# One core: another order of the steps in pooled attention with two gated MLPs

## The chip, the core and the metric

The kernel runs on one core of one Trainium2 chip. The metric is the device time of one execution in microseconds. In the views of the profile PE is TensorE's matrix unit, PEld its weight loads, DVE is VectorE, ACT is ScalarE, POOL is GpSimd and SP is SyncE, which issues the DMAs. A span runs from the first instruction to the last.

## The reference

Three stages follow one another on 8 batches of 576 rows and 512 columns.

```python
# attention, 8 heads of 64: keys and values are means over 8 rows (576 -> 72)
scores = scale * np.matmul(q, k_p.transpose(0, 1, 3, 2))
scores = scores - np.max(scores, axis=-1, keepdims=True)
attn = np.exp(scores)
attn = attn / (np.sum(attn, axis=-1, keepdims=True) + 1e-09)
x = np.matmul(attn, v_p)                  # then heads side by side
# first MLP, 512 -> 1024 -> 512
h = np.maximum(x @ w_in, 0.0)
conv_out = ...                            # 3 taps along the rows, per column
x = h * (1.0 / (1.0 + np.exp(-conv_out))) @ w_out
# second MLP, 512 -> 2 x 512 -> 512
h = gelu_tanh(x @ w_in)
u, v = (h[..., :d_ff // 2], h[..., d_ff // 2:])
v_n = (v - mu) / np.sqrt(var + 1e-06) * g_ln
v_s = np.einsum('ts,bsd->btd', w_sg, v_n) + b_sg[None, :, None]
out = x + (u * v_s) @ w_out
```

## The kernel before

**Precision.** Every large product is made from high and low parts: a tile is cast on ACT to the short form, the rest is subtracted into a second tile (`subtract`, L134, on DVE or POOL), and three matmuls take the place of one (`mm3`, L99 to L101, `mm_sum`, L106, `three` and `passes`, L746). Some weights arrive as 64-bit numbers; `to_f32` makes f32 of them with three DVE instructions on integers (L146, L149, L152).

**Tasks.** The work is cut into tasks, each a generator of steps. A step is named by the letter of its task, an index and a batch, as `u1.4`. For the places below:

- `k`, `K`, `v`, `V`: load and pool keys and values; `p`, `q`: transposes of q (DVE, L403); `s`: scores and softmax (matmuls L418, DVE L431); `e`: transposes of the exponentials and their split (ACT cast L502, L134); `a`: attention output.
- `i`, `t`: loads and conversions of the weights of the first MLP; `I`: its input product (PE L106 into `psi`), relu (ACT L557), taps (ACT L567, DVE L569 and L570), tanh (ACT L572), gate (DVE L576), cast and low part (ACT L579, POOL L134); `O`: its output product (PE L99 to L101 into `pso`, evacuated at L601 and L603 into `ob`, stored to `x2s` in DRAM).
- `y` (`t_x2`): the stored result is loaded as `xb` (SP, L675) and transposed by DVE (L681, two halves). `T` (`t_xc`): for seven products, a POOL subtraction of quarters (L693), an ACT cast (L698) and the low part (L134).
- `n` and `u` (`t_v2`, `t_u`): the second MLP's products for v and u, each with seven products instead of eight (Strassen and Winograd's scheme). `products` sets their steps: matmuls 1, 5, copy, 6, 2, copy, 7, add, copy, 4, add, 3 and the last evacuations. Three ACT copies (L769 for `n`, L813 for `u`, into `tmp`) must be made before the next product is accumulated in the same bank; three DVE adds (L774, L823) and gelus on ACT (L771, L777, L778, L820, L826, L827) close it. For v follow statistics on DVE (L783, L784), the inverse deviation on POOL (L787, L788) and the normalisation on DVE (L791, two of 128x512).
- `g`, `G`, `H`, `l`: the spatial weights and the last ones (conversions by `to_f32`). `S` (`t_sc`): quarters of v for the spatial product (POOL L927, ACT L616, DVE L134). `d` (`t_sp`): the spatial product with the same scheme, its evacuations on DVE (L976) and the multiplication with u on POOL (L980). `o`: the output product and the residual.

**Banks.** PSUM has three banks called `psa`, two `psi` and three `pso`, so a product waits until the bank's earlier user has been evacuated.

**Order.** A string `ORDER` with 3617 keys lists the steps. The function `step` advances the generator of a key by one step and ties each instruction that this issues to the one before on the same engine:

```python
        for n in range(seen[0], len(issued)):
            ins = issued[n]
            if ins.engine in last:
                tc.add_manual_dep(ins, last[ins.engine], pin, reason="order")
            last[ins.engine] = ins.name
```

So the string alone sets the order on every engine's queue, SP's with its DMAs among them. Between engines only data and buffers order the work.

Of the kernel before, what the change touches and what calls it, by code (L numbers as in the profile page):

```python
# [26 lines left out]
def pooled_attention_gated_mlps(  # L27
# [25 lines left out]
    B, H, S, D = q.shape  # L53
# [35 lines left out]
    def a_bank():  # L89
        return psum1.tile([128, 512], F32, tag="a", bufs=3, name="psa")  # L90
# [45 lines left out]
    def to_f32(raw, t, tmp=None):  # L136

        w = raw.rearrange("p (n t) -> p t n", t=2)
        lo, up = w[:, 0, :], w[:, 1, :]
        ti = t.bitcast(U32)
        mi = ti if tmp is None else tmp.bitcast(U32)
        nc.vector.tensor_scalar(out=mi, in0=up, scalar1=3, scalar2=0x3FFFFFF8,  # L146
                                op0=ALU.logical_shift_left, op1=ALU.bitwise_and)
        yield
        nc.vector.scalar_tensor_tensor(out=mi, in0=up, scalar=0xC0000000, in1=mi,  # L149
                                       op0=ALU.bitwise_and, op1=ALU.bitwise_or)  # L150
        yield
        nc.vector.scalar_tensor_tensor(out=ti, in0=lo, scalar=29, in1=mi,  # L152
                                       op0=ALU.logical_shift_right, op1=ALU.bitwise_or)
        yield
# [82 lines left out]
    def staged(name, n, where=None):  # L237

        if where is not None:
            p_, tag, size = where  # L240
            early[name] = [p_.tile([128, size], F32, tag=tag, name=name), 0]
        z, at = early[name]
        early[name][1] += 512 * n
        return z[:, at:at + 512 * n].rearrange("p (a s) -> p a s", a=n)

    def pool_sum(eng, raw, dst, n):
        a = raw[0:n]
        if eng is nc.vector:
            eng.tensor_reduce(out=dst, in_=a.rearrange("p a (r d) -> p a d r", r=POOL), axis=AX.X, op=ALU.add)
            return  # L250
        eng.tensor_tensor(out=a[:, :, 0:256], in0=a[:, :, 0:256], in1=a[:, :, 256:512], op=ALU.add)
        yield
        eng.tensor_tensor(out=a[:, :, 0:128], in0=a[:, :, 0:128], in1=a[:, :, 128:256], op=ALU.add)
        yield
        eng.tensor_tensor(out=dst, in0=a[:, :, 0:64], in1=a[:, :, 64:128], op=ALU.add)

    kv = {}

    def t_k(i, b):

        n = (2, 2, 1)[i]
        P = 128 if i < 2 else 64
        if b > 1:
            raw = att2.tile([128, 2, 512], F32, tag="raw", name="raw")
        else:
            raw = staged(f"st{b}", n, ((in1, "xh", XW * KC), (slot, "hg", 2 * NF * CH))[b] if i == 0 else None)
        rows_ = k[b].rearrange("h (j r) d -> (h j) (r d)", r=POOL)[256 * i:256 * i + P * n]
        nc.sync.dma_start(out=raw[0:P, 0:n], in_=rows_.rearrange("(a p) x -> p a x", p=P))
        yield
        if b == 1:  # L270
            kv["k1", i] = raw
            return
        if ("kp", b) not in kv:
            kv["kp", b] = att1.tile([128, 5, D], F32, tag="kp", name="kp")
        eng = dve if b == 0 and i != 1 else pool
        yield from pool_sum(eng, raw[:, 0:n], kv["kp", b][0:P, 2 * i:2 * i + n, :], P)
# [332 lines left out]
    w2 = {}  # L609
# [15 lines left out]
    wf, wc = {}, {}  # L625

    def t_w2(i, *_):
        kt, e = i % KC, i // KC
        p = w2["p"]
        raw = p.tile([128, 1024], U32, tag=f"c{e}{4 + kt % 3}", name="w2raw")  # L630
        for c in range(4):
            r0 = 128 * c + 32 * kt
            nc.sync.dma_start(out=raw[32 * c:32 * c + 32], in_=w_in2[r0:r0 + 32, 1024 * e:1024 * e + 1024])
        yield
        if kt % 2 == 0:
            wf[e, kt // 2] = p.tile([128, 2, 512], F32, tag=f"c{e}{kt // 2}", name="w2f")
        yield from to_f32(raw, wf[e, kt // 2][:, kt % 2, :], a_bank())
# [301 lines left out]
    g2 = {}  # L939
# [112 lines left out]
    def step(key):  # L1052

        if key not in running:
            i, _, b = key[1:].partition(".")
            running[key] = iter(tasks[key[0]](int(i or 0), int(b or 0)) or ())
        more = next(running[key], 0)
        issued = nc.cur_bb.bb.instructions
# [5 lines that stand above are left out]
        seen[0] = len(issued)  # L1064
        return more is None

    for key in ORDER.split():
        step(key)
# [30 lines left out]
```

## Time and profile before

| What | Value |
|---|---|
| median of 3 runs | 979.6 us |
| lowest, highest | 978.8, 980.35 us |
| profiled execution | 980.6 us |
| its span | 978.8 us |
| its mean granted clock of TensorE | 0.988 |
| PE busy | 925.9 us (95%) |
| DVE busy | 785.7 us (80%) |
| POOL busy | 564.1 us (58%) |
| ACT busy | 530.4 us (54%) |

The span falls into stages: the opening with the first batch's attention and the loads of weights (0 to 57 us), the start of the first MLP (57 to 137), its steady part (137 to 540), the passage to the second MLP (540 to 577), the products for u and v (577 to 760), the start of the spatial gating (760 to 800), its steady part and the end (800 to 979). A share of busy time over the whole span mixes these, so the views below are read by stage. In the view of windows a granted clock of 1.00 is 2.4 GHz and 0.50 is 1.2 GHz.

### The profile page before, as it was taken

How to read it: one execution, taken by the hardware profiler on the slowest of the kernel's cores; microseconds unless marked ns; L12 is line 12 of the kernel's file. 1: busy time of each engine (PE TensorE's matmuls, PEld its weight loads, DVE VectorE, ACT ScalarE, POOL GpSimd, SP SyncE). 2: the span in 40 equal slices, each digit the busy share in tenths (PEclk: the TensorE clock that was granted, in tenths of full speed). 3: DMA queues.
4: the chain of work that ended last, by engine and by line, in shares of the span. 5: the costliest groups of instructions: out<-in, count | busy, mean ns of one | idle time of the engine just before them, and what ended most of it. 6: DMA issues, size and time to landing. Idle time of an engine off the chain costs nothing.

```text
span 978.8 us, 15842 instructions
## 1 busy us (share of the span) xinstructions
PE 925.9 (95%) x5396; PEld 843.8 (86%) x5396; DVE 785.7 (80%) x1399; ACT 530.4 (54%) x1108; POOL 564.1 (58%) x630
## 2 busy tenths in 40 slices
PE   5888899999999999999999899999999899999998
PEld 5677789989898998988899689998899889989996
DVE  5889997879788688787877469898786889797774
ACT  3656677676667576675656356655556333233211
POOL 3777797777968575475253265643653655554430
PEclk9899999999999999999999999999999999999999
DMA  9975183646746255132710685476437565566453
GB/s 236 266 225 98 47 182 105 156 142 155 186 112 164 85 138 137 49 95 68 198 40 1 121 166 131 137 209 149 124 125 231 187 211 180 148 213 185 163 175 129
DMA packets 182701, 143.61 MB, mean 147 GB/s; under 512 B 99776, under 2 KB 136924, under 8 KB 182620
## 3 DMA queue, kind: packets, MB, share of 16 engines
q1 hardware_dynamic: 182620, 142.61, 54.0%
q8 instruction: 42, 0.69, 0.3%
q14 instruction: 39, 0.32, 0.1%
HBM read 94.20 MB, written 48.37 MB: 146 GB/s over the span
## 4 chain that ended last, share of the span: by engine, by line
PE 68%; DVE 14%; DMA 8%; SPq 4%; issue 3%; ACT 2%; POOL 2%; DVEq 0%; ACTq 0%; POOLq 0%
PE psi L106 18%; PE psa L746 9%; PE pso L746 8%; PE pso L99 6%; PE pso L101 6%; PE pso L100 6%; PE psi L100 3%; PE psi L99 3%; PE psi L101 3%; DMA xb<-x2s 3%; PE psa L418 3%; PE psa L106 3%; DMA st<-in_v_dram 1%; DMA qb<-in_q_dram 1%; DVE sc L134 1%
## 5 line engine op out<-in xcount | busy, mean ns | idle before, releaser
L134 POOL TENSOR_TENSOR hg<-g,hg 128x384 fp32r<-128x384 f32 x96 | 100.9, 1057 | 77.9 <-ACT hg L579 77.2
L980 POOL TENSOR_TENSOR u<-u,tmp 128x288 f32<-128x288 f32 x64 | 61.1, 971 | 76.7 <-DVE tmp L976 67.6
L569 DVE SCALAR_TENSOR_TENSOR psi<-h,coef,psi 128x384 f32<-128x384 f32 x96 | 58.9, 614 | 31.3 <-ACT psi L567 30.7
L557 ACT ACTIVATE h<-psi 128x386 f32<-128x386 f32 (+1 forms) x96 | 47.4, 493 | 56.8 <-PE psi L106 56.5
L693 POOL TENSOR_TENSOR xb<-xb 128x768 f32<-128x768 f32 x24 | 45.7, 1905 | 47.5 <-DVE xc L134 21.4
L572 ACT ACTIVATE psi<-psi 128x384 f32<-128x384 f32 x96 | 46.0, 480 | 47.7 <-DVE psi L570 47.2
L134 POOL TENSOR_TENSOR eTl<-xb,eTh 128x512 fp32r<-128x512 f32 (+1 forms) x30 | 46.4, 1545 | 43.9 <-ACT eTh L502 41.4
L616 ACT CAST sc<-vf 128x512 fp32r<-128x512 f32 x48 | 28.9, 619 | 63.3 <-POOL vf L927 29.0
L570 DVE SCALAR_TENSOR_TENSOR psi<-h,coef,psi 128x384 f32<-128x384 f32 x96 | 59.8, 623 | 3.4
L576 DVE SCALAR_TENSOR_TENSOR g<-psi,h 128x384 f32<-128x384 f32 x96 | 52.2, 544 | 11.4 <-ACT psi L572 9.5
L418 PE MATMUL psa<-KBT,qT 128*128 128x144 f32 (+1 forms) x320 | 53.5, 300 | 7.0 <-DVE e L431 2.8
L418 PEld LDWEIGHTS psa<-KBT,qT 128*128 128x128 f32 (+1 forms) x320 | 45.0, 184 | 15.4 <-issue 5.7
L567 ACT ACTIVATE psi<-h,coef 128x384 f32<-128x384 f32 x96 | 56.3, 586 | 3.1
L579 ACT CAST hg<-g 128x384 fp32r<-128x384 f32 x96 | 47.7, 506 | 15.2 <-DVE g L576 13.7
L746 PE MATMUL psa<-xc,wc 128*128 128x384 f32 x252 | 51.5, 350 | 4.5 <-DVE xc L134 2.4
L746 PE MATMUL pso<-wc,xc 128*128 128x256 f32 x378 | 52.0, 285 | 3.8 <-POOL xc L134 2.1
L746 PE MATMUL psa<-wc,xc 128*128 128x256 f32 x378 | 51.7, 284 | 3.7 <-ACT tmp L769 2.3
L746 PEld LDWEIGHTS pso<-wc,xc 128*128 128x128 f32 x378 | 49.0, 190 | 5.2 <-ACT tmp L769 2.5
L746 PEld LDWEIGHTS psa<-wc,xc 128*128 128x128 f32 x378 | 49.1, 189 | 4.8 <-ACT tmp L769 3.1
L746 PE MATMUL pso<-xc,wc 128*128 128x384 f32 x252 | 48.6, 338 | 3.3 <-ACT tmp L813 2.0
L746 PEld LDWEIGHTS psa<-xc,wc 128*128 128x128 f32 x252 | 44.8, 196 | 6.5 <-DVE xc L134 2.7
L995 ACT CAST g<-u 128x256 fp32r<-128x256 f32 x64 | 22.1, 403 | 45.8 <-POOL u L980 35.2
(396 smaller groups left out, 3130.1 us busy)
## 6 DMA issues: line engine op xcount, KB each, us to landing
xb<-eds SPq DMA_DIRECT2D x24, 384.0 KB, 3.1
x2s<-ob SPq DMA_DIRECT2D x36, 256.0 KB, 2.3
xb<-x2s SPq DMA_DIRECT2D x48, 192.0 KB, 5.1
us<-ub SPq DMA_DIRECT2D x24, 384.0 KB, 2.7
vs<-vg SPq DMA_DIRECT2D x18, 512.0 KB, 4.8
u<-us SPq DMA_DIRECT2D x16, 576.0 KB, 5.9
vf<-vs SPq DMA_DIRECT2D x16, 512.0 KB, 4.2
out_dram<-ob SPq DMA_DIRECT2D x32, 256.0 KB, 2.5
```

The costliest lines, as they stand in the source:

```text
L99: nc.tensor.matmul(out=out_, lhsT=ah, rhs=bh, start=first, stop=False)
L100: nc.tensor.matmul(out=out_, lhsT=al, rhs=bh, start=False, stop=False)
L101: nc.tensor.matmul(out=out_, lhsT=ah, rhs=bl, start=False, stop=last)
L106: nc.tensor.matmul(out=out_, lhsT=a, rhs=b_, start=(i == 0), stop=(i == n - 1))
L134: eng.tensor_tensor(out=out, in0=in0, in1=hi.bitcast(F32), op=ALU.subtract)
L418: nc.tensor.matmul(out=ps[0:n, 2 * SP * x:2 * SP * x + 2 * SP], lhsT=qT[:, p, 0:n], rhs=KBT[:, p, :], start=True, stop=True)
L567: nc.scalar.activation(out=y, in_=tap(1), func=AF.Copy, scale=cw(1, f))
L569: nc.vector.scalar_tensor_tensor(out=y, in0=tap(0), scalar=cw(0, f), in1=y, op0=ALU.mult, op1=ALU.add)
L570: nc.vector.scalar_tensor_tensor(out=y, in0=tap(2), scalar=cw(2, f), in1=y, op0=ALU.mult, op1=ALU.add)
L576: nc.vector.scalar_tensor_tensor(out=go, in0=y, scalar=1.0, in1=tap(1), op0=ALU.add, op1=ALU.mult)
L746: nc.tensor.matmul(out=ps, lhsT=a, rhs=b_, start=first and i == 0, stop=last and i == n - 1, skip_group_check=True)
L980: pool.tensor_tensor(out=z, in0=z, in1=o, op=ALU.mult)
```

## The change

The string `ORDER` is replaced by one with the same 3617 steps in another order; the steps of one task keep their own sequence. Every engine runs the same instructions as before (PE 5148, DVE 1399, ACT 1106, POOL 627 and SP 625 in the program). Most steps move by a few places. Two more edits issue no instruction: in `t_k` a tile is noted before the first pause of the step instead of after it, and in `t_w2` a tile is made by whichever of two steps comes first; they let some steps stand in another order. Lines below them have a number higher by one in the changed kernel.

```diff
-ORDER = '''z k0.0 k1.0 k2.0 z z p0.0 c p1.0 p2.0 v0.0 v1.0 p3.0 p4.0 v2.0 i0 i1 z z k0.1 k1.0 p0.1 t3 k0.0 p0.0 k1.0 i2
...
+ORDER = '''z k0.0 k1.0 k2.0 z z p0.0 c p1.0 p2.0 v0.0 v1.0 p3.0 p4.0 v2.0 i0 i1 z z k0.1 p0.0 p0.0 i3 p0.1 k1.0 k1.0 k1.0
...
@@ t_k @@
-        yield
         if b == 1:
             kv["k1", i] = raw
+        yield
+        if b == 1:
             return
...
@@ t_w2 @@
-        if kt % 2 == 0:
+        if (e, kt // 2) not in wf:
```

Three places follow. A row is an instruction with the tiles that it writes and reads; a number behind a name tells tiles of that name apart.

**The transition.** On DVE, where the second MLP's first input `xb` is transposed and split into `xc`, before:

```order
L681 STREAM_TRANSPOSE xb_6118<-xb_6118 128x768 x2
L681 STREAM_TRANSPOSE xb_6126<-xb_6126 128x768
L134 TENSOR_TENSOR xc_6132<-xb_6118,xc_6132 128x768
L681 STREAM_TRANSPOSE xb_6126<-xb_6126 128x768
L134 TENSOR_TENSOR xc_6164<-xb_6118,xc_6164 128x768
L134 TENSOR_TENSOR xc_6198<-xb_6118,xc_6198 128x768
L843 STREAM_TRANSPOSE wsg_6178<-wsg_6178 128x576
```

and now:

```order
L682 STREAM_TRANSPOSE xb_6102<-xb_6102 128x768 x2
L134 TENSOR_TENSOR xc_6135<-xb_6102,xc_6135 128x768
L682 STREAM_TRANSPOSE xb_6110<-xb_6110 128x768 x2
L134 TENSOR_TENSOR xc_6158<-xb_6102,xc_6158 128x768
L134 TENSOR_TENSOR xc_6161<-xb_6102,xc_6161 128x768
L602 TENSOR_SCALAR ob_6206<-pso_6080 128x512
L844 STREAM_TRANSPOSE wsg_6208<-wsg_6208 128x576
```

The low part of the first split stands between the transposes of the two halves of the input instead of behind three of them, and the evacuation of the output product (L602) stands ahead of the weights' transpose.

**The products, at 684 to 690 us of the trace.** On DVE, with the statistics and normalisation of v (`vg`), the adds of u (`ub`) and the input of the next batch (`xb`, `xc`), before:

```order
L784 BN_AGGR mv_7584<-st_7583 128x2
L681 STREAM_TRANSPOSE xb_7461<-xb_7461 128x768
L823 TENSOR_TENSOR ub_7621<-pso_7574,tmp0_7551 128x384
L134 TENSOR_TENSOR xc_7618<-xb_7531,xc_7618 128x768
L791 TENSOR_SCALAR vg_7414<-vg_7414,mv_7584,rstd_7623 128x512 x2
L774 TENSOR_TENSOR vg_7589<-psa_7638,tmp0_7610 128x256
L823 TENSOR_TENSOR ub_7662<-pso_7521,tmp2_7626 128x384
```

and now:

```order
L785 BN_AGGR mv_7596<-st_7595 128x2
L134 TENSOR_TENSOR xc_7611<-xb_7553,xc_7611 128x768
L824 TENSOR_TENSOR ub_7614<-pso_7568,tmp0_7551 128x384
L792 TENSOR_SCALAR vg_7413<-vg_7413,mv_7596,rstd_7601 128x512 x2
L682 STREAM_TRANSPOSE xb_7537<-xb_7537 128x768
L775 TENSOR_TENSOR vg_7579<-psa_7626,tmp0_7616 128x256
L775 TENSOR_TENSOR vg_7579<-psa_7604,tmp2_7649 128x256
```

The last transpose of `xb` has moved from ahead of the normalising pair to behind it, and the statistics that stood between the transposes are further ahead. On ACT at 711 to 717 us, with the copies of u's bank (L813, now L814) and the cast of the next input (L698, now L699), before:

```order
L813 COPY tmp0_7918<-psa_7904 128x384
L698 CAST xc_7927<-xb_7920 128x768
L813 COPY tmp1_7951<-psa_7904 128x384
L771 ACTIVATE vg_7824<-pso_7825 128x256
L777 ACTIVATE vg_7824<-vg_7824 128x256
```

and now:

```order
L814 COPY tmp0_7925<-psa_7906 128x384
L814 COPY tmp1_7940<-psa_7906 128x384
L699 CAST xc_7949<-xb_7895 128x768
L772 ACTIVATE vg_7820<-pso_7821 128x256
L814 COPY tmp2_7962<-psa_7906 128x384
```

The second copy has passed the cast, and the third one the gelu at L778. On PE five of the pairs in which the product 4 stood right behind the product 7 of the same bank have other products between them, and three such pairs are new.

**The start of the spatial gating.** On DVE from 770 to 778 us, with the evacuations L976 (now L977), the low parts of the spatial input (`sc`) and a weight conversion (L146), before:

```order
L976 SCALAR_TENSOR_TENSOR tmp_8638<-pso,coef,bsg 128x288
L976 SCALAR_TENSOR_TENSOR tmp_8638<-pso,coef,tmp_8638 128x288
L976 SCALAR_TENSOR_TENSOR tmp_8581<-pso,coef,bsg 128x288
L134 TENSOR_TENSOR sc<-vf,sc 128x512
L976 SCALAR_TENSOR_TENSOR tmp_8626<-psa,coef,tmp_8626 128x288
L134 TENSOR_TENSOR sc<-vf,sc 128x512
L976 SCALAR_TENSOR_TENSOR tmp_8546<-psa,coef,bsg 128x288
L134 TENSOR_TENSOR sc<-vf,sc 128x512
L976 SCALAR_TENSOR_TENSOR tmp_8611<-pso,coef,tmp_8611 128x288
L146 TENSOR_SCALAR t<-T4raw 128x512
L134 TENSOR_TENSOR sc<-sf,sc 128x512
```

and now:

```order
L977 SCALAR_TENSOR_TENSOR tmp_8638<-pso,coef,bsg 128x288
L977 SCALAR_TENSOR_TENSOR tmp_8638<-pso,coef,tmp_8638 128x288
L134 TENSOR_TENSOR sc<-sf,sc 128x512
L134 TENSOR_TENSOR sc<-vf,sc 128x512
L977 SCALAR_TENSOR_TENSOR tmp_8585<-pso,coef,bsg 128x288
L134 TENSOR_TENSOR sc<-vf,sc 128x512
L977 SCALAR_TENSOR_TENSOR tmp_8632<-psa,coef,tmp_8632 128x288
L134 TENSOR_TENSOR sc<-vf,sc 128x512
L977 SCALAR_TENSOR_TENSOR tmp_8529<-psa,coef,bsg 128x288
L134 TENSOR_TENSOR vr<-vf,vr 64x512
L977 SCALAR_TENSOR_TENSOR tmp_8587<-psa,coef,tmp_8587 128x288
L146 TENSOR_SCALAR t<-T4raw 128x512
```

The low part that is taken from `sf` has moved to the front, behind the second evacuation into `tmp`, and the conversion L146 stands further back. On SP the loads of the next batch's v for the gating now stand ahead of the loads of the residual.

Elsewhere: in the opening one weight load of the first MLP's output side (`t3`) moves back behind others, some (`i3`, `i5`, `i6`) move forward, and two DVE instructions (a coefficient's and a weight's) move back. In the start of the first MLP the scores' product `s0.1` stands before a block of the input product on PE, and the DVE transpose of `p2.2` stands ahead of two attention steps. In the steady part of the first MLP one gate (`I6.9`) moves forward, and one (`I1.7`) now stands behind a subtraction of the exponentials (`e0.6`) on DVE.

## Rows read from the trace of the kernel before

**Rows 1.** Windows: window, length, busy PE, PEld, DVE, ACT, POOL, clock, DMA share

```profile
0.00:30.00 30.00, 18.52 (x121) 15.81 (x122) 19.66 (x40) 12.20 (x30) 12.46 (x32) 0.95 1.07 247
30.00:57.00 27.00, 24.59 (x166) 20.59 (x166) 21.49 (x41) 17.03 (x44) 20.36 (x26) 0.86 1.06 280
57.00:137.00 80.00, 69.79 (x412) 60.73 (x410) 76.31 (x141) 50.67 (x110) 61.42 (x84) 1.00 0.49 109
137.00:540.00 403.00, 400.87 (x2138) 363.23 (x2139) 326.92 (x597) 267.13 (x535) 261.38 (x310) 1.00 0.45 118
540.00:577.00 37.00, 31.02 (x143) 26.59 (x142) 18.62 (x23) 13.97 (x24) 17.45 (x11) 0.91 0.73 134
577.00:760.00 183.00, 172.89 (x1191) 168.46 (x1191) 152.00 (x258) 109.91 (x229) 89.53 (x75) 1.00 0.56 159
760.00:800.00 40.00, 34.77 (x225) 32.27 (x224) 37.12 (x68) 12.40 (x28) 21.39 (x21) 0.96 0.56 173
800.00:979.00 179.00, 173.48 (x1011) 156.16 (x1009) 133.56 (x237) 47.05 (x114) 80.08 (x74) 0.99 0.56 177
```

**Rows 2.** The same windows view around TensorE's half clock

```profile
27.20:34.10 6.90, 6.80 (x38) 5.28 (x38) 5.74 (x12) 5.13 (x15) 5.03 (x9) 0.51 1.11 224
774.80:778.20 3.40, 1.43 (x11) 1.19 (x9) 3.40 (x5) 1.13 (x3) 3.40 (x4) 1.00 0.23 83
778.20:781.60 3.40, 3.02 (x12) 3.02 (x13) 3.37 (x5) 0.62 (x3) 3.40 (x3) 0.50 0.00 0
```

**Rows 3.** Waits of PE in 577 to 760: total us, times, longest

```profile
PE psa L746 <- ACT tmp L769: 2.3, 4, 0.7
PE pso L746 <- ACT tmp L813: 2.0, 3, 1.0
PE psa L746 <- DVE vg L774: 1.5, 1, 1.5
```

**Rows 4.** Timeline: start, length, engine, line, tiles, idle before and releaser; 677 to 691

```profile
677.01 0.99 DVE L791 TENSOR_SCALAR vg<-vg,mv,rstd 128x512 f32<-128x512 f32 x2
...
686.89 2.49 DVE L791 TENSOR_SCALAR vg<-vg,mv,rstd 128x512 f32<-128x512 f32 x2
687.05 4.02 POOL L693 TENSOR_TENSOR xb<-xb 128x768 f32<-128x768 f32 x2 [1.15 <-DVE xc L134]
...
690.23 0.96 PE L746 MATMUL pso<-xc,wc 128*128 128x384 f32 x4 [1.32 <-DVE ub L823]
```

**Rows 5.** Timeline, ACT and PE, 714 to 717

```profile
714.75 0.83 ACT L698 CAST xc<-xb 128x768 fp32r<-128x768 f32 x1 [3.21 <-DVE xb L681]
...
716.02 1.15 PE L746 MATMUL psa<-xc,wc 128*128 128x384 f32 x5 [1.21 <-ACT tmp L813]
```

**Rows 6.** Timeline, DVE and PE, 772 to 779

```profile
772.22 0.52 DVE L976 SCALAR_TENSOR_TENSOR tmp<-pso,coef,bsg 128x288 f32<-128x288 f32 x1 [1.50 <-POOL u L980]
...
777.24 1.28 DVE L134 TENSOR_TENSOR sc<-sf,sc 128x512 fp32r<-128x512 f32 x1
...
778.58 1.57 PE L746 MATMUL psa<-sgc,sc 128*128 128x288 f32 x5 [2.35 <-DVE sc L134]
```

**Rows 7.** Timeline of the transition: DVE, POOL and PE

```profile
554.68 0.98 DVE L681 STREAM_TRANSPOSE xb<-xb 128x768 f32<-128x768 f32 x1 [1.99 <-DMA xb<-x2s]
...
557.66 2.40 POOL L693 TENSOR_TENSOR xb<-xb 128x768 f32<-128x768 f32 x1 [1.83 <-DMA wsg<-in_moe_w_sg_dram]
...
568.43 0.86 PE L746 MATMUL pso<-wc,xc 128*128 128x256 f32 x5 [2.13 <-POOL xc L134]
```

**Rows 8.** Waits of PE in 57 to 137

```profile
PE psa L418 <- DVE e L431: 2.8, 2, 2.3
PE psa L418 <- DVE qT L403: 2.2, 1, 2.2
```

**Rows 9.** Timeline, DVE, 57 to 60

```profile
57.43 2.48 DVE L146 TENSOR_SCALAR t<-w0raw 128x512 uint32<-128x512 uint32 x1 [1.73 <-POOL wi6hl L134]
```

**Rows 10.** Timeline, DVE, 366 to 371

```profile
366.89 3.51 DVE L134 TENSOR_TENSOR eTh<-xb,eTh 32x256 fp32r<-32x256 f32 x1
```

More of the change, by code (lines that the diff above doesn't have):

```diff
@@ L268, in t_k @@
         nc.sync.dma_start(out=raw[0:P, 0:n], in_=rows_.rearrange("(a p) x -> p a x", p=P))
+        if b == 1:
+            kv["k1", i] = raw
         yield
         if b == 1:
-            kv["k1", i] = raw
             return
```

2 lines of the change are left out of this document (1 added, 1 removed).

## The prediction

> **What bounds the kernel now.** I read the profile in this order: busy time of each engine by stage, the granted clock of TensorE around its pauses, what PE waits for in each stage, and then the timeline at the longest of those waits.
>
> The stages [rows 1] show PE as the bound nearly everywhere: it is busy for 400.87 of 403 us in the steady part of the first MLP, 172.89 of 183 in the products of the second, and 173.48 of 179 in the spatial gating. The change adds and removes no instruction, so PE's busy time at full clock stays, and there are only two things to win: time in which PE stands still, and time in which it runs at half clock. Length less busy time gives PE's idle time by stage: 11.5 us in 0–30, 2.4 in 30–57, 10.2 in 57–137, 2.1 in 137–540, 6.0 in 540–577, 10.1 in 577–760, 5.2 in 760–800 and 5.5 after, 53 us in all. Two stages have another bound beside PE: in 57–137 the DVE is busy for 76.31 of 80 us, and in 760–800 for 37.12 of 40. There PE waits because DVE is full, so a swap helps only if it makes DVE's work shorter or brings forward the one result that PE lacks.
>
> The clock adds to it. After PE was busy for 1.43 of 3.40 us, the next 3.40 us ran at a granted 0.50, that is 1.2 GHz instead of 2.4 [rows 2]; 6.90 us of the opening ran at 0.51. Half of a 3.4 us stretch in which PE works all the time is 1.7 us lost, on top of the wait before it. PE was at work for 3.02 us of that gated stretch, so it cost some 1.5.
>
> **The change part by part.** Every engine runs its instructions in the order of the steps, so a step that moves takes all that it issues with it. The sum is made against the profiled execution (980.6 us, span 978.8), which lies 1.0 above the median of 979.6.
>
> *The products, 577–760.* PE's waits there [rows 3] are mostly for evacuations, the copies of ACT and the adds of DVE that free a PSUM bank. Three of them stand behind something that had no need to go first.
> First [rows 4]: PE starts at 690.23 after 1.32 us of waiting for DVE's add L823, which stood behind the normalising pair L791. That pair takes 0.99 us where POOL is quiet (677.01) and took 2.49 at 686.89, with POOL's subtractions L693 starting at 687.05: 1.50 us more. POOL could begin because DVE had done the last transpose for them just before. In the new order that transpose comes behind the pair, so POOL cannot have begun when the pair runs. The add then ends some 1.5 us sooner and the 1.32 goes.
> Second [rows 5]: ACT's copy that PE awaits at 716.02 (1.21 us) stood behind the cast at 714.75, which had itself waited 3.21 us for DVE's transposes. The new order has the copy in front of the cast: 1.21 goes. Third, PE's longest wait for a copy of L813 into the other bank, 1.0 [rows 3]: this copy now precedes two gelus on ACT, and 1.0 goes. Together 3.5 us.
> Smaller ones: four waits for the copies of L769 make 2.3 us [rows 3]; PE waits about half a microsecond wherever a product that needs the copy of a bank stands directly behind the product before it in that bank. Five such pairs get other products between them (−2.5 at 0.5 each) and three new ones arise (+1.5): −1.0. The remaining moves of this stage bring waits and take them, at about this size; I put them at zero. Term −4.5; from −8, if the 1.5 us wait on L774 [rows 3] and 2 us of the small ones go too, to 0, if each wait is replaced.
>
> That a DVE instruction with two SBUF inputs and a POOL instruction delay one another is shown by [rows 4]. The Trainium skill, "SBUF — State Buffer", section "Who interferes with whom", gives the reason as a port pair that one instruction holds to its end, and adds that whichever issues first holds it: the order of issue decides who is blocked. The 2.49 against 0.99 agrees with that. This rule also speaks against the change: the order is fixed within each engine only, and which of two engines comes first is decided on the chip. By it the 1.32 could come back at the next pair, and the term would be −3.2 instead of −4.5.
>
> *Spatial gating begins, 760–800.* PE waits 2.35 us at 778.58 for the low part of a split that DVE makes at 777.24, and then runs 3.4 us at half clock [rows 2, 6]. DVE had been idle for 1.50 us before 772.22, and the inputs of that low part were there. In the new order it stands ahead, in this idle time, and the weight conversion L146 comes later. The wait and its half-clock stretch are worth 2.35 + 1.5 = 3.9 us. But DVE has only 2.9 us of idle time in this stage [rows 1]; 1.50 of it is now filled by work that left a full stretch, so DVE gets 1.5 us ahead, and what is next late is a later L976. I take half of the 3.9: −2. Bounds: −4.5 (the wait, the stretch and a little more) and +1 (POOL is at work in just that idle time, and a meeting costs 1.50 as in [rows 4]).
> On SP's queue the next batch's loads go ahead of the residual loads here; those are needed 30 us later and their transfer costs nothing.
>
> *The transition, 540–577.* DVE waited 1.99 us for a load at 554.68 [rows 7]; the low part of the first split now fills this, and the second transposes come about 1 us sooner, with them POOL's subtraction at 557.66 (from there 10.8 us of POOL, ACT and DVE work in series lead to PE's product at 568.43, which waited 2.13). On PE two blocks of the output projection now stand before the first product instead of behind: that moves the waits and takes none away. Term −1, the 1 us on the serial chain; −3 if one of its half-clock stretches goes with it (1.5 to 2), +3 if the moved waits add a stretch and a further POOL collision.
>
> *The DVE-bound start, 57–137.* PE's long waits are 2.8 on L431 and 2.2 on a transpose of q [rows 8]. The transpose now stands ahead of two attention steps on DVE, which takes about half of the 2.2 (−1.1). The product of the scores that waits for the pooled keys moves before a block of input-projection work on PE, so that several waits merge into one of about 3 us; that wins nothing and invites a half-clock stretch (+1.7 at the 1.7 above, taken at a third: +0.5). DVE's excess decides the rest: the conversion at 57.43 took 2.48 us beside POOL [rows 9], five times the 0.5 of one L791. I see as many of these meetings move as vanish: −0.5. Term −1; from −7 (two thirds of the 10.2 us of idle time) to +6 (four more meetings at 1.5).
>
> *The opening, 0–57.* Weight loads and pooling steps change places with DMA share at 1.06 to 1.07 [rows 1], so the bytes set the pace and the sum of bytes is the same. A load that is needed late moves behind others, and two DVE conversions leave the front of the queue: −1, with −4 if half the 6.90 us stretch runs at full clock and +2 if a load that was early is now awaited.
>
> *Steady stretches, 137–540 and 800–979.* PE idles 2.1 and 5.5 us there [rows 1]. One gate step moves forward, another now stands behind a DVE subtraction that took 3.51 us [rows 10]: zero, from −1.5 to +4 (that 3.51 in full, once).
>
> The two edits outside the table issue no instruction and cost nothing.
>
> Sum: −4.5 − 2 − 1 − 1 − 1 + 0 = −9.5; 980.6 − 9.5 = 971.1 on the profiled execution, 970.1 on the median: **970 us**.
>
> **The rivals.** *More goes than I count.* If the order really lets DVE and POOL miss each other in the DVE-bound stages, 57–137 gives −7, 760–800 −4.5, the opening −2 and the products −6.5: −20, 959.5. For it: each stage holds more idle time than that [rows 1]. Against: DVE's idle time of 3.7 and 2.9 us says that work, not waiting, fills these stages.
>
> *The waits only move, and the order does not do what it says.* Where PE waits for one evacuation the next is rarely early, and a POOL instruction delayed by 1 us meets another DVE instruction. Each of the 3.5 us in the products then comes back at the next bank and the full DVE passes its delays on. −1 in all: 978.6. For it: waits on L769, L813 and L823 recur in small pieces [rows 3]. Against: the three named waits each have a cause that the new order takes away.
> The rule on the order of issue in the Trainium skill ("SBUF — State Buffer", "Who interferes with whom") would lead here: by it an order per engine cannot keep two engines apart.
>
> *Slower: DVE meets POOL more often in 57–137.* POOL is busy for 61.42 of those 80 us, DVE runs 141 instructions there with 3.7 us to spare, and PE waits for DVE. Each further meeting costs 1.5 us [rows 4], and beyond 3.7 us all of it falls on PE. With my other terms at −8.5 it needs (8.5 + 3.7) / 1.5 = 8 further meetings to come out level; 13 give 19.5 − 3.7 − 8.5 = +7, 987.
>
> **How the numbers follow.** Forecast (−9.5 give or take 4) 0.50; more goes 0.17; waits only move 0.17; slower 0.16. A measurement of this kernel can tell some 0.2% (2 us) from no change. Faster: 0.50 + 0.17 + 0.04 of the third case = 0.71; within: 0.11 of the third; slower: 0.16 + 0.02 = 0.18. The range runs from 959 (which cuts the lower part of the second case, 0.07) to 982 (which cuts most of the fourth, 0.13).
>
> **What would show it.** Right: no DVE L791 pair near 687 above 1.2 us and no PE wait over 1 us on L823 or L813 in 577–760, PE's idle time there at 5 to 6 us instead of 10.1; no wait over 1.5 us on an L134 of the spatial gating in 760–800; PE busy time in 137–540 as before. Wrong: DVE's busy time in 57–137 above 77 with PE's idle time above 10.2 there; a new half-clock stretch in 57–137; a PE wait of 3 us in the steady part; or idle time that is gone from 577–760 and found again in 760–800.

## The result, and the profile after

The changed kernel takes 966.46 us (median of 4 runs, 965.48 to 966.96) where the kernel before takes 979.31 on the same chip: a ratio of 0.9866, interval 0.9849 to 0.9883, or 12.8 us less. The forecast was 970, with a range from 959 to 982. A second measurement of the changed kernel gave 966.14 and 0.9846 (0.9833 to 0.9860). Its profiled execution took 966.23 us with a span of 964.3.

The view of windows, cut so that each window holds the same matmuls as the stages in [rows 1] (the first window joins two of them; columns as there):

```profile
0.00:55.90 55.90, 41.20 (x285) 35.30 (x286) 40.58 (x80) 28.72 (x72) 32.45 (x59) 0.94 1.08 259
55.90:136.00 80.10, 72.26 (x414) 62.86 (x413) 72.50 (x142) 50.73 (x110) 61.38 (x83) 0.98 0.50 115
136.00:537.30 401.30, 400.58 (x2138) 362.98 (x2137) 328.16 (x597) 267.89 (x535) 260.95 (x312) 1.00 0.46 118
537.30:572.20 34.90, 30.05 (x145) 26.26 (x144) 19.95 (x24) 13.60 (x23) 15.58 (x10) 0.90 0.83 144
572.20:746.90 174.70, 171.23 (x1190) 168.11 (x1188) 147.61 (x258) 108.66 (x229) 91.60 (x75) 1.00 0.56 164
746.90:786.70 39.80, 35.16 (x225) 32.65 (x224) 33.22 (x64) 13.34 (x30) 20.16 (x19) 0.96 0.63 193
786.70:964.30 177.60, 172.90 (x1011) 156.04 (x1009) 134.37 (x241) 46.40 (x114) 80.69 (x76) 1.00 0.56 175
```

The lengths against [rows 1] are the result in one table:

| Stage | before | after | difference | forecast |
|---|---|---|---|---|
| opening | 57.0 | 55.9 | −1.1 | −1 |
| start of the first MLP | 80.0 | 80.1 | +0.1 | −1 |
| first MLP, steady | 403.0 | 401.3 | −1.7 | 0 |
| transition | 37.0 | 34.9 | −2.1 | −1 |
| products | 183.0 | 174.7 | −8.3 | −4.5 |
| start of the gating | 40.0 | 39.8 | −0.2 | −2 |
| gating, steady, and the end | 178.8 | 177.6 | −1.2 | 0 |
| span | 978.8 | 964.3 | −14.5 | −9.5 |

Each column is one execution. Where the clock falls, one order does not repeat to 1 us: in five other executions with the old order in the opening (products only, both forms of the three waits, less work, isolated waits, below) PE comes out of it 1.0 to 1.9 us earlier than in the profile before. The −1.1 there can't be told from this.

In the products PE's idle time fell from 10.1 to 174.70 − 171.23 = 3.5 us. PE's waits there, which answer [rows 3] (total, times, longest):

```profile
PE pso L747 <- ACT tmp L770: 1.5, 2, 1.0
PE psa L747 <- ACT tmp L770: 1.0, 2, 0.5
PE pso L747 <- ACT tmp L814: 0.6, 1, 0.6
PE psa L747 <- ACT tmp L814: 0.2, 1, 0.2
```

No add of DVE holds PE there any more. The place of [rows 4], on DVE and POOL in the timeline:

```profile
675.08 1.00 DVE L792 TENSOR_SCALAR vg<-vg,mv,rstd 128x512 f32<-128x512 f32 x2 [0.44 <-POOL rstd L789]
676.00 0.97 DVE L682 STREAM_TRANSPOSE xb<-xb 128x768 f32<-128x768 f32 x1
677.11 3.78 POOL L694 TENSOR_TENSOR xb<-xb 128x768 f32<-128x768 f32 x2 [2.06 <-DVE xb L682]
```

The normalising pair runs while POOL still waits for the transpose behind it, and takes 1.00 instead of 2.49 us.

At the start of the gating the wait of 2.35 us in [rows 6] is gone, and two others stand in its place (timeline of DVE and PE):

```profile
757.24 1.00 DVE L134 TENSOR_TENSOR sc<-sf,sc 128x512 fp32r<-128x512 f32 x1
758.89 1.33 DVE L134 TENSOR_TENSOR sc<-vf,sc 128x512 fp32r<-128x512 f32 x1 [0.66 <-ACT sc L617]
...
760.58 0.85 DVE L134 TENSOR_TENSOR sc<-vf,sc 128x512 fp32r<-128x512 f32 x1
761.35 0.51 DVE L977 SCALAR_TENSOR_TENSOR tmp<-psa,coef,tmp 128x288 f32<-128x288 f32 x1
...
761.91 1.06 PE L747 MATMUL psa<-sgc,sc 128*128 128x288 f32 x6 [1.67 <-DVE tmp L977]
...
767.66 0.52 DVE L977 SCALAR_TENSOR_TENSOR tmp<-psa,coef,bsg 128x288 f32<-128x288 f32 x1 [0.69 <-POOL u L981]
...
768.33 0.90 PE L747 MATMUL psa<-sgc,sc 128*128 128x288 f32 x5 [1.90 <-DVE tmp L977]
```

PE needs the evacuation L977 at 761.35. It stands behind low parts, one of which waited 0.66 us for its cast. The second wait ends with the evacuation at 767.66, which itself waited 0.69 us for a multiplication of POOL. DVE's busy time in this stage fell from 37.12 to 33.22 us, and the stage got shorter by only 0.2. One execution is not enough for this stage: in the second profiled one of the changed kernel there is no half-clock stretch here, and the stage takes 39.0 us:

```profile
747.70:786.70 39.00, 33.49 (x225) 31.15 (x224) 34.44 (x64) 13.29 (x29) 20.27 (x20) 1.00 0.64 198
```

PE waits 1.15, 1.90 and 1.38 us for L977 there.

In the start of the first MLP the merged wait came (timeline of PE):

```profile
62.44 0.76 PE L419 MATMUL psa<-KBT,qT 128*128 128x144 f32 x4 [2.03 <-DVE KBT L298]
```

Behind it came a stretch at a lower clock (windows view):

```profile
61.00:64.40 3.40, 1.96 (x9) 1.96 (x10) 3.27 (x7) 0.47 (x1) 2.06 (x4) 0.84 0.28 67
64.40:67.80 3.40, 3.40 (x18) 3.40 (x18) 1.97 (x5) 2.52 (x5) 1.42 (x3) 0.66 0.49 136
```

### The profile page after: what moved, and what is told of

Its sections match the earlier page's. It is cut to its first block, busy times and chain, and to the rows that moved or that the text cites. A ratio compares the mean times of both kernels' runs of the same rounds, so it can differ in the third digit from the quotient of the medians.

```text
span 964.3 us, 15821 instructions
## 1 busy us (share of the span) xinstructions
PE 923.4 (96%) x5396; PEld 844.2 (88%) x5396; DVE 776.4 (81%) x1399; ACT 529.3 (55%) x1108; POOL 562.8 (58%) x630
## 4 chain that ended last, share of the span: by engine, by line
PE 75%; POOL 8%; DVE 8%; issue 3%; DMA 2%; ACT 2%; SPq 1%; POOLq 0%; DVEq 0%; ACTq 0%
PE psi L106 18%; PE psa L747 13%; PE pso L747 12%; PE pso L99 5%; PE pso L101 5%; PE pso L100 5%; PE psi L99 3%; PE psi L100 3%; PE psi L101 3%; PE psa L106 3%; PE psa L419 3%; POOL raw L251 1%; POOL xb L694 1%; POOL en L449 1%; DVE t L152 1%
## 5 line engine op out<-in xcount | busy, mean ns | idle before, releaser
L134 POOL TENSOR_TENSOR hg<-g,hg 128x384 fp32r<-128x384 f32 x96 | 100.3, 1053 | 74.2 <-ACT hg L580 68.0
L134 POOL TENSOR_TENSOR eTl<-xb,eTh 128x512 fp32r<-128x512 f32 (+1 forms) x30 | 46.4, 1545 | 32.9 <-ACT eTh L503 32.8
L699 ACT CAST xc<-xb 128x768 fp32r<-128x768 f32 x42 | 34.6, 835 | 23.1 <-DVE xb L682 11.9
L457 POOL TENSOR_TENSOR en<-e,rs 128x512 f32<-128x512 f32 (+1 forms) x30 | 32.0, 1066 | 24.4 <-ACT hg L580 10.1
```

The lines of the kernel that those rows point to most:

```text
L134: eng.tensor_tensor(out=out, in0=in0, in1=hi.bitcast(F32), op=ALU.subtract)
```

## The experiments

Steps are written as task, index, batch and, behind #, the step of the task. To see where an order gains, each trace was laid beside that of the kernel before: the start of every matmul there, less its start in the profile before, and the median over a stretch. These are the differences in us (one profiled execution each), by the time in the kernel before:

| Stretch | changed | products only | all but products | three places | three waits | two repairs | isolated waits | single moves |
|---|---|---|---|---|---|---|---|---|
| 40–60 | −0.9 | −1.5 | −0.7 | −0.8 | −1.2 | −1.0 | −0.8 | −1.1 |
| 140–160 | −1.5 | −0.8 | −1.1 | −1.8 | −0.4 | +1.6 | +1.6 | −3.2 |
| 520–540 | −2.7 | −0.4 | −2.3 | −3.1 | −0.2 | +0.3 | +0.2 | −3.9 |
| 580–600 | −4.9 | +6.1 | −4.2 | −1.5 | −0.3 | +4.0 | −1.3 | −5.9 |
| 740–760 | −13.1 | −1.9 | −4.4 | −8.1 | −1.2 | −3.6 | −1.0 | −14.2 |
| 800–820 | −13.5 | −2.2 | −5.2 | −8.4 | −1.0 | −3.1 | −0.1 | −15.5 |
| 940–960 | −14.5 | −2.1 | −6.2 | −9.4 | −0.9 | −4.1 | −1.1 | −16.5 |

**The products stage alone, and all but it.** The two orders were joined step by step: up to the stage the old one, in it the new one, behind it the old one, and the reverse. The first steps at the joint:

```diff
-y0.1#1 n0.0#11 y0.1#2 u0.0#13 g3#0 G#0 H5#0 ... u1.0#0 T1.1#0 u1.0#1 ...
+y0.1#1 ... g3#0 ... g3#1 ... n0.0#11 ... G#0 n0.0#12 y0.1#2 u1.0#0 u0.0#13 u1.0#1 ... T1.1#0 ... u1.0#2 ...
```

> The order of the kernel before, with the new order for the steps of the products stage alone (577 to 760 us of the kernel before). The profile after shows this stage 8.3 us shorter (174.7 against 183.0 for the same 1190 matmuls). If the stage gains by its own order, the kernel comes out 8.3 us below before: about 971. If part of the 8.3 was handed over by earlier stages (a better state of the queues at the stage's entry), less: 4.5 us as forecast, about 975.

> The complement: the new order everywhere but in the products stage, which keeps the old one. If the stages add up, it stands 13.1 - 8.3 = 4.8 us below before, about 974.5. If the stages depend on one another, e1 and e2 together gain clearly less or more than 13.1 us.

The first: 977.91 us, ratio 0.9964 (0.9951 to 0.9977). The second: 973.75, ratio 0.9922 (0.9907 to 0.9938). Together 3.6 + 7.8 = 11.4 thousandths against 13.4 for the whole, so most adds up, but the share of the first came out far below 8.3 us. The table shows why: from 580–600 to 740–760 this kernel goes from +6.1 to −1.9, an 8.0 us gain inside the stage, as the changed kernel's 8.2, and the second kernel gains 0.2 there. The stage's gain is its own. What hides it in the total is a loss of 6.5 us at the joint. The timeline of the first kernel there, on DVE, ACT and PE:

```profile
581.79 0.78 DVE L844 STREAM_TRANSPOSE wsg<-wsg 128x576 f32<-128x576 f32 x1 [5.17 <-DMA wsg<-in_moe_w_sg_dram]
582.49 0.94 DVE L682 STREAM_TRANSPOSE xb<-xb 128x768 f32<-128x768 f32 x1
...
583.46 0.83 ACT L699 CAST xc<-xb 128x768 fp32r<-128x768 f32 x1 [4.83 <-DVE xb L682]
584.20 0.47 ACT L814 COPY tmp<-psa 128x384 f32<-128x384 f32 x1
...
584.72 1.65 PE L747 MATMUL psa<-xc,wc 128*128 128x384 f32 x4 [4.31 <-ACT tmp L814]
```

One transpose of weights, not needed for long, headed DVE's queue and waited 5.17 us for its load. The next transpose waited behind it, ACT's cast for that, the copy L814 behind the cast, and PE for the copy: 4.31 us, through three engines' queues. Behind this wait PE ran at half clock (windows view), which fits the rest of the loss:

```profile
583.10:589.80 6.70, 5.08 (x20) 5.08 (x21) 5.09 (x9) 3.83 (x9) 2.02 (x2) 0.50 0.30 117
```

**Three named waits.** In the kernel before, with the rest of the order as it was:

```diff
-T1.4#0 y1.4#2 u1.3#7 n0.3#16 u1.3#8 T1.4#1 n0.3#17 u1.3#9
+T1.4#0 u1.3#7 n0.3#16 u1.3#8 T1.4#1 n0.3#17 y1.4#2 u1.3#9
...
-n1.0#14 n2.0#7 O5.10#1 T7.1#1 u0.1#2
+n2.0#7 O5.10#1 u0.1#2 T7.1#1 n1.0#14
...
-T1.5#0 T1.5#1 T5.5#0 T7.5#0 n0.4#11 u1.4#3 u1.4#4 u1.4#5
+n0.4#11 u1.4#3 u1.4#4 u1.4#5 T1.5#0 T1.5#1 T5.5#0 T7.5#0
```

In a first form only the low part T1.5#1 went behind the copy, and so behind the subtraction T5.5#0 that overwrites its input; that part of the computation differs there. The cast T1.5#0 stayed ahead of the copy, so this form tests two of the three waits.

> The order of the kernel before with four steps moved: the last transpose of xb behind the normalising pair (y1.4), the third copy of u's bank ahead of two gelus and a cast (u0.1), and ahead of a cast (u1.4). These are the three waits that the forecast named, 1.32 + 0.96 + 1.21. If each has the cause named, the pair takes 1.0 instead of 2.49 us, the three waits go and the kernel gains 3.5 us: about 975.8. By the rival, that waits only move and that issue order brings DVE and POOL together again at the next instruction, the same time turns up as new waits within a few us of each place, and the gain is under 1 us.

It gave 980.23 us, ratio 0.9996 (0.9985 to 1.0007). PE gets ahead by 0.8 us at the pair, waits 1.32 at the copy behind the cast, and 1.02 more for a copy of L770 some 4 us later; the stage loses 1.3 in all. The form shown above:

> The order of the kernel before with the three named waits of the products stage taken away by moving steps: the last transpose of xb behind the normalising pair (y1.4); the third copy of u's bank ahead of two gelus and a cast (u0.1); the cast for T1.5 and POOL's two subtractions behind it after the copy (u1.4). In the run before this one two of these three moves stood alone: the pair fell to 1.09 us and its wait from 1.32 to 0.50, the wait at u0.1 went and another of 0.57 came 1.2 us later. By the forecast's step all 3.5 us are gained. By what that run showed, about half comes back at the next evacuation: 1.5 to 2 us.

979.34 us, ratio 0.9986 (0.9976 to 0.9996): 1.4 us. The stage's waits of PE:

```profile
PE psa L747 <- ACT tmp L770: 2.3, 4, 0.7
PE psa L747 <- DVE vg L775: 2.0, 2, 1.5
PE pso L747 <- ACT tmp L770: 2.0, 4, 0.6
PE pso L747 <- ACT tmp L814: 1.0, 2, 0.6
PE psa L747 <- DVE ub L824: 0.4, 1, 0.4
PE pso L747 <- DVE ub L824: 0.4, 1, 0.4
```

The causes were the right ones: at the three places PE gets ahead by 1.1, 0.9 and 1.4 us, and the pair takes 1.00 us here too (0.39 of its wait of 1.32 stays). But new waits follow close behind: 0.57 on L775 and 0.2 within 3 us of the first, 0.4 some 10 us after the second, 0.57 on L770 within 3 us of the third, and the stage as a whole gains 0.9 (from −0.3 to −1.2 in the table). Of the 3.4 us gained at the places 2.5 were lost again in the stage. The new order keeps them and 5 us more; there, what stands behind each place has moved too.

**Three places of the changed kernel, by hand.** Shortened to the steps that matter:

```diff
-T3.0#0 T5.0#0 T7.0#0 T2.0#0 T2.0#1 T5.0#1 ... O7.11#1 ... n0.0#0 n0.0#1 n0.0#2 u0.0#0
+T5.0#0 T7.0#0 ... O7.11#1 ... T2.0#0 T5.0#1 ... n0.0#0 u0.0#0 n0.0#1 T6.0#1 ... T3.0#0 ... n0.0#2
...
-d1.0#12 S2.1#1 S6.1#0 d0.0#9 d0.0#10 ... S3.1#0 S6.1#1 ... S6.1#2 ... d0.1#2 d0.1#3 S3.1#2
+S6.1#0 d0.0#9 d1.0#12 d0.0#10 ... S2.1#1 ... S6.1#2 ... d0.1#2 d0.1#3 R0.1#1 S3.1#0 ... S3.1#2
...
-s0.1#0 I1.0#0 t1#1 t1#2 I0.0#4 ... s0.1#2 s0.1#3 ... I2.0#0
+I1.0#0 s0.1#0 I0.0#4 ... s0.1#2 ... t1#1 t1#2 I1.0#1 I2.0#0 s0.1#3
```

> The changed kernel with three stretches put in another order by hand. (a) Transition: the evacuation O7.11 on ACT ahead of two casts, u0.0's first product ahead of n0.0's second, POOL's subtraction for T4 behind the low part of T6. In the profile after PE waits 2.92 and 1.58 us here. (b) Start of the gating: DVE's evacuations d0.0 and d0.1 ahead of low parts of splits, POOL's S6.1 ahead of two multiplications and S3.1 behind two. PE waits 1.67 and 1.90 us here. (c) Start of the first MLP: I1.0 and I2.0 on PE around s0.1, the gate I0.0 ahead of a weight conversion; PE waits 2.03 us here and a half-clock stretch follows. If DVE's amount of work bounded (b) and (c), as the forecast held, these two gain nothing and the kernel only gets (a)'s 2 to 4 us: about 963.5. If an instruction that heads a queue and waits is what holds PE there, (b) gives 2 to 3.5 and (c) 1.5 to 3 more: about 959.

972.38 us, ratio 0.9908 (0.9894 to 0.9922), slower than the changed kernel by some 4 us. Each wait aimed at shrank, and each time another took its place. In the transition PE began its first product without a wait and waited 2.4 us (0.93 + 1.45) for the second, where the changed kernel waits 4.5. Then it stood for 1.07 and 1.23 us at copies that ACT had behind casts, and for 0.92 at a copy that ACT had behind two gelus, one of which waited for DVE: 520–540 to 580–600 goes from −3.1 to −1.5, where the changed kernel gains 2.2. At the start of the first MLP the 2.03 became one of 2.23 for the copy p2.1. In the gating 1.67 became 0.25 and 1.90 became 0.41, and this came 5 us later:

```profile
773.77 0.69 DVE L134 TENSOR_TENSOR sc<-vf,sc 128x512 fp32r<-128x512 f32 x1 [1.82 <-ACT sc L617]
774.38 0.51 DVE L977 SCALAR_TENSOR_TENSOR tmp<-psa,coef,bsg 128x288 f32<-128x288 f32 x1
...
774.94 1.06 PE L747 MATMUL psa<-sgp,sc 128*128 128x288 f32 x6 [2.41 <-DVE tmp L977]
...
777.76 3.21 PE L747 MATMUL pso<-sgc,sc 128*128 128x288 f32 x12 [1.49 <-DVE tmp L977]
```

POOL's subtraction S3.1 had moved back, its low part on DVE had not, and the evacuation that PE needs stood behind that low part while it waited 1.82 us.

**The repair.** With these queue heads put right (against the order of the run above):

```diff
-n0.0#2 u0.0#2 T7.0#1
+n0.0#2 u0.0#2 T6.0#1 T6.0#2 ... T7.0#1 ... u0.0#5 ... n0.0#5 T4.0#1 T4.0#2
...
-S3.1#2 d0.1#4 d0.1#5 d0.1#6 l3#2 ... l2#3 d1.1#2
+d0.1#4 d0.1#5 d0.1#6 S3.1#2 d1.1#2 l3#2 ... l2#3
...
-t1#1 t1#2 I1.0#1 I2.0#0 ... s0.1#5 t1#5 s1.1#3 t6#0 I1.0#2 I1.0#3 ... s0.1#6 p2.1#2
+I1.0#1 I1.0#2 I2.0#0 s0.1#3 I1.0#3 ... p2.1#2 t0#4 I1.0#4 s0.1#5 s1.1#3 t1#1 ... t1#3 s0.1#6
```

> The changed kernel with the three stretches of the run on three places ordered anew. (a) Transition: POOL's T6 ahead of T7, the first copies of n0.0 and u0.0 ahead of the cast for T6, T4's cast behind two copies, u1.0's copy ahead of the cast for T1.1. (b) Gating: as in that run, but with the low part S3.1 and the conversions behind the evacuations d0.1 and d1.1. (c) Start of the first MLP: as in that run, but with the copy p2.1 ahead of I1.0's tanh, and the taps of I1.0 ahead of a conversion. If the lost time there was due to a queue's head waiting for something that PE did not yet need, each stretch gains against the profile after: (a) 2, (b) 2.5, (c) 1: about 961. If what bounds these stretches is the chain of loads, subtractions and casts itself, no order gains and it stays at 966 or above.

976.51 us, ratio 0.9951 (0.9939 to 0.9963): worse still. Two lines hold most of it:

```profile
77.08 1.12 PE L479 MATMUL psa<-ident,en 128*128 128x128 f32 x4 [4.68 <-POOL en L449]
...
581.70 1.84 DVE L682 STREAM_TRANSPOSE xb<-xb 128x768 f32<-128x768 f32 x2 [6.33 <-DMA xb<-x2s]
```

At 77 us PE waits 4.68 for the normalisation of the exponentials. On POOL it stands behind the low part of t1, which waited 3.38 us for ACT's cast and through it for DVE's conversion, and behind another low part and two pooling sums; on DVE the sum that it needs (s0.1#6) had gone behind three conversions. At 581 DVE waits for the load y0.1, which cannot start until the buffer of the batch before is free. That buffer's last reader is T4's low part, which ends at 573.8 instead of 565.5 in the changed kernel; the load is issued right behind it in both. The transposes of y0.1 end at 583.5, where the changed kernel has them done at 573.5. PE waits 3.18 us for this at 585.87, behind ACT's cast.

**Less work for DVE.** In the kernel before, two of the last weights' tiles:

```diff
-        nc.vector.scalar_tensor_tensor(out=mi, in0=up, scalar=0xC0000000, in1=mi,
-                                       op0=ALU.bitwise_and, op1=ALU.bitwise_or)
+        if whole:
+            nc.vector.scalar_tensor_tensor(out=mi, in0=up, scalar=0xC0000000, in1=mi,
+                                           op0=ALU.bitwise_and, op1=ALU.bitwise_or)
...
-        return weight(p, tag, w_out2[128 * i:128 * i + 128, :], dve, None, lambda hl: wo2.__setitem__(i, hl))
+        return weight(p, tag, w_out2[128 * i:128 * i + 128, :], dve, None, lambda hl: wo2.__setitem__(i, hl), i < 2)
```

> The kernel before, with two of the three integer instructions of the conversions left out for two of the four tiles of the last weights: four instructions of 0.68 to 0.69 us, all on DVE between 783 and 788 us. The values of these weights are then not those of the reference. The forecast held that 760 to 800 is bound by the amount of DVE's work (37.1 of 40 us). Then the stage shrinks by about 2.7 us: 978.3 on a before of 981. If a single late instruction holds PE, only the wait of 1.43 at 788.6 can go, and the wait of 2.35 at 778.6, which lies ahead of these four, stays: 0 to 1.4 us.

979.17 us, ratio 0.9983 (0.9972 to 0.9994). The stage with the same 225 matmuls, and PE's waits in it:

```profile
759.30:798.10 38.80, 33.89 (x225) 30.99 (x225) 35.79 (x64) 12.36 (x28) 21.38 (x21) 1.00 0.61 185
```

```profile
PE psa L748 <- DVE sc L134: 2.3, 1, 2.3
PE psa L748 <- DVE tmp L978: 1.8, 3, 1.1
PE pso L748 <- DVE tmp L978: 0.6, 1, 0.6
```

Of 2.8 us of DVE work left out the stage gives back 40.0 − 38.8 = 1.2. The wait of 2.3 on L134, which lies ahead of the four instructions, is untouched, the 1.43 is gone and one of 1.1 is new (behind a low part `gr` on DVE that took 2.10 us instead of 0.49). But the clock differs too: the half-clock stretch of [rows 2] did not come here. The run on isolated waits (below) has the old order in this stage and no such stretch either:

```profile
759.00:799.90 40.90, 34.34 (x225) 30.80 (x224) 37.77 (x68) 12.44 (x28) 21.02 (x21) 1.00 0.55 168
```

Against this one, in which a low part took 2.52 us instead of 1.43, the stage is 2.1 us shorter, with 2.0 us less of DVE's busy time. In the kernel before DVE works without a gap from 772.2 us to the evacuation for which PE waits the 1.43 us at 788.6; the run on isolated waits, at full clock, waits 1.91 for the same one. Here that evacuation comes 2.6 us earlier against the instructions ahead of it. So this run does not rule out that the amount of DVE's work bounds the stage; for this part of it, it speaks for it.

**Isolated waits.** In the kernel before:

```diff
-I7.9#0 I7.9#1 I7.9#2 a3.7#4 ... O0.9#0 I6.9#3 I6.9#4
+I7.9#0 I6.9#3 I7.9#1 I6.9#4 I7.9#2 a3.7#4 ... O0.9#0
...
-e0.6#4 O7.4#7 I1.7#3 I1.7#4
+O7.4#7 I1.7#3 I1.7#4 e0.6#4
...
-S7.4#2 R0.4#0 S6.4#1 S6.4#2
+R0.4#0 S6.4#1 S6.4#2 S7.4#2
```

> The order of the kernel before with five steps moved, outside the products stage, at the three waits of PE which the new order takes away in the steady stretches: I6.9's tanh and gate ahead of I7.9's steps (0.91 us at 474.9), the gate I1.7 ahead of the subtraction e0.6 that took 3.51 us (0.76 at 371.0), the low part S6.4 ahead of S7.4 (0.71 at 857.6). The forecast put these stretches at zero; the profile after shows them 1.7 and 1.2 us shorter. If a lone wait with slack behind it is worth its length, all 2.4 us are gained: 978.2 on a before of 980.6. If waits move on here as they did in the products (a third to a half stayed gained), 1 us.

977.55 us, ratio 0.9967 (0.9957 to 0.9978). Laid beside the kernel before, PE gets ahead by 0.5 at 371 us, 0.9 at 475 and 1.0 at 857, 2.3 us of the 2.4, and keeps it to the end of the stages but for 0.2 us. The same kernel lost 2.6 us near 65, where its order is that of the kernel before (below), and gained 1.5 in the transition, where it is too.

**Single moves on the changed kernel.**

```diff
-T4.4#1 n0.4#2
+n0.4#2 T4.4#1
...
-t4#1 I4.0#5 t4#2 t4#3 t7#0 I4.0#6 I5.0#3 t4#4 t4#5 s4.1#6 e3.1#2
+e3.1#2 t4#1 I4.0#5 t4#2 t4#3 t7#0 I4.0#6 I5.0#3 t4#4 t4#5 s4.1#6
...
-e2.0#1 p4.0#2
+p4.0#2 e2.0#1
...
-s0.1#0 I1.0#0 t1#1 t1#2 I0.0#4 ... I2.0#0 ... s0.1#6 p2.1#2
+I1.0#0 s0.1#0 I0.0#4 ... t1#1 t1#2 ... I2.0#0 ... p2.1#2 ... s0.1#6
```

> The changed kernel with four waits of PE taken away by short moves: the copy n0.4 ahead of the cast T4.4 (1.02 us), the subtraction e3.1 ahead of a conversion (1.34), the copy p4.0 ahead of e2.0's (0.48 of 1.59), and around s0.1 the order of the run on three places with the copy p2.1 ahead of the tanh (2.03, of which that run gained 0.4 because a wait of 2.23 for p2.1 came behind). At full value 3.9 us: 962.5 where the changed kernel has 966.5. If the next wait gives back half, 964.5. If the loads and conversions moved aside are missed later, 966.5 or more.

966.01 us, ratio 0.9854 (0.9840 to 0.9869). Its span is 962.3. It was run once more beside the changed kernel on one chip:

> The changed kernel once more, beside the kernel with single moves on the same chip. A ratio to before of 0.985 to 0.988 as in its first measurement. Its profile shows how far the waits of one order repeat from execution to execution: in the steady stretches within 0.1 us, in the opening and at s0.1 (62 us) within 2 us.

> The changed kernel with the four short moves, once more, for the comparison on one chip. By the two profiles its span is 2.0 us shorter (962.3 against 964.3). If that is its worth, it stands 2 us (0.2%) below the changed kernel of the same job; if the difference comes from the opening's and the clock's variation, the two are equal.

The changed kernel: 966.14 us, 0.9846 (0.9833 to 0.9860), span 964.5. The single moves: 965.13, 0.9843 (0.9829 to 0.9856), span 962.4. Both profiles of each agree to 0.2 us and differ by 2.1, but the medians differ by 1.0 us with intervals that cover each other, so the two count as equal. In the second profile of the changed kernel each of PE's waits in the products is the same to 0.01 us; the half-clock stretches are not in the same places (last section). The start of the first MLP gains (79.5 us at a clock of 1.00 against 80.1 at 0.98); behind e3.1 the 1.34 us is gone and PE waits 1.86 at a1.1 instead of 0.28.

## Why the prediction was right, and where its steps were not

The sign, the time and the main mechanism hold: PE's waits in the products went, by the order of evacuations. The sum came out 5 us too small in the spans and 3.3 us in the medians, and its terms erred both ways. Of its signs of being wrong one came: a new half-clock stretch in the start of the first MLP.

**Products (−4.5, measured −8.3, beyond the bound of −8).** The three named waits did have the causes named, and are gone. Two readings on the way were not exact: [rows 4] names the low part L134, not a transpose, as what POOL waited for last, though in the new order it is the transpose that holds POOL off (2.06 us); and the pair there is a TENSOR_SCALAR with one tensor as input, so that row does not show a DVE instruction with two. The mis-sized terms are three. The small moves that were put at zero took away 3.1 us of waits (0.40, 0.54, 1.45 and 0.72 in the kernel before) and brought one of 1.02: −2.1. The pairs gave −1.4 instead of −1.0. With the 3.5 of the three these are 7.0 us, less 0.4 by which shorter gaps grew: the 6.6 by which PE's idle time fell. And a wait costs more than its length: in the kernel before, the matmul behind each of the 14 waits over 0.2 us took 0.10 us longer to its successor than the usual spacing; nine such waits fewer are 0.9 us. The last 0.8 is PE's busy time too (172.89 and 171.23, with one matmul less in the window) and was not traced further. DVE was busy for 4.4 us less in this stage (152.00 and 147.61), which fits fewer meetings with POOL; how much of the gain this is was not separated.

**The rival "waits only move"** is right for moves one at a time: three of them kept 0.9 us of 3.5. It failed for the whole order. The rival "more goes" (its 979.6 − 20 makes 959.6) had the products at −6.5, nearer than the forecast, and the two stages with a full DVE at −7 and −4.5, where +0.1 and −0.2 came. The Trainium skill's rule on the order of issue ("SBUF — State Buffer", "Who interferes with whom") agrees with the pair at 675.08, 1.00 us with POOL held off. It did not lead to the lost gain that the rival drew from it: what gave the time back in the runs was a wait in line, behind casts and low parts.

**Start of the gating (−2, measured −0.2).** The low part moved ahead, and its wait of 2.35 went, as forecast; DVE got 3.9 us of busy time back. The mis-sized term is what is late next, the later L976, for which half of the 3.9 was taken off: PE waited 1.67 and 1.90 us for two L977, and the half-clock stretch came again (0.96 over the stage in both). In the three other profiled executions with this order in the stage (the second one of the changed kernel, both of the single moves) the stretch did not come, the 1.90 did, and the stage gained 1.1 to 1.5 us. So some 1 us of what is missing does not repeat from one execution to the next. The premise that DVE's amount of work bounds the stage stays open: in the new order DVE is idle for 6.6 of the 39.8 us, 3.31 of them in one gap behind PE's last wait, but in the old one the stage gave back 2.1 us for 2.8 us of work left out, at the same clock.

**Start of the first MLP (−1, measured +0.1).** PE's idle time fell here, from 10.2 to 7.8 us (2.23 became 0.73 at p2.2). The step that was mis-sized is the half-clock stretch counted at a third, +0.5: it came (0.66 behind the merged wait of 2.03 us), and PE's busy time grew from 69.79 to 72.26 us, with two matmuls more in the window. That spent the gain. DVE's busy time fell by 3.8 us; what this gave by itself was not separated.

**Transition (−1, measured −2.1)** was within its bounds. The two blocks that moved ahead on PE did move the wait (2.92 and 1.58 us ahead of n0.0), to evacuations of the output product. The size is not sure: the runs on less work and on isolated waits, with the old order here, are 1.5 us shorter than the profile before as well. **Opening (−1, −1.1)** agrees by luck, since the old order's other executions come out 1.0 to 1.9 us ahead there too.

**Steady stretches (0, measured −1.7 and −1.2).** The step that failed is the price of 3.51 for the subtraction at 366.89: in the new order the same subtraction takes 1.36, so the wait of 0.76 goes instead of growing. The other two waits (0.91 and 0.71) were left uncounted. The isolated moves show that such waits, with slack behind them, are worth their full length.

## What to carry to other kernels

Price a wait by what stands behind it: one that stands alone in a stage with slack is worth its whole length (2.3 of 2.4 us here), one among dense evacuations a quarter of it when it is moved alone (0.9 of 3.5). When a step is moved, follow the instruction behind it on every queue that it was moved past, and the buffer that it frees: a head of a queue that waits for a load costs PE its wait through two other engines (4.31 us at a joint of two good orders). A busy share of over 90% is no proof of a bound. Taking work away from that engine is a test of it, if the runs that are compared had the same granted clock: 2.8 us less work was worth 1.2 us against a run with a half-clock stretch and 2.1 against one without.

## What the runs showed that was not expected

The granted clock does not follow from the order alone. Two kernels with the order of the kernel before in this stretch, with alike waits ahead (2.06 and 1.81 us, 2.10 and 1.97), were granted different clocks; the isolated waits first, the three waits below (windows view):

```profile
61.00:64.40 3.40, 1.86 (x11) 1.54 (x9) 3.33 (x5) 0.50 (x2) 3.14 (x5) 1.00 0.15 41
64.40:67.80 3.40, 1.89 (x12) 1.54 (x12) 3.30 (x7) 1.25 (x3) 1.55 (x3) 0.79 0.89 240
67.80:71.20 3.40, 2.58 (x10) 2.60 (x11) 3.26 (x8) 2.71 (x6) 2.27 (x3) 0.50 0.58 204
```

```profile
61.00:64.40 3.40, 1.42 (x8) 1.10 (x7) 3.30 (x7) 0.91 (x2) 3.04 (x6) 1.00 0.34 84
64.40:67.80 3.40, 1.74 (x12) 1.52 (x12) 3.30 (x7) 1.25 (x4) 1.28 (x1) 1.00 0.98 250
67.80:71.20 3.40, 2.90 (x18) 2.74 (x19) 3.30 (x8) 2.71 (x6) 2.29 (x3) 1.00 0.51 155
```

The first ran at 0.50 where PE was busier before, the second at 1.00, and the first came out of this stretch about 2 us later (+1.6 against −0.5 at 70 to 80 us). The changed kernel differs from itself in the same way. Its first profile has half-clock stretches at 63 and 770 us and none at 102. Its second has one at 102 and none at 63 or 770. Ahead of this one PE waited 1.33 us, and in the first profile 1.34. The second profile's window, then the first's:

```profile
102.20:105.60 3.40, 3.40 (x12) 2.96 (x11) 2.17 (x5) 1.19 (x3) 3.32 (x7) 0.51 0.00 0
102.20:105.60 3.40, 3.34 (x21) 2.99 (x21) 3.27 (x8) 1.42 (x4) 3.32 (x7) 1.00 0.00 0
```

A term of 1 us for the opening, for this stage, for the transition or for the start of the gating is therefore below what one profiled execution can show.
